# Weighting and folding two of eight value-cache parts on VectorE and GpSimd ahead of TensorE

## The chip, the cores and the metric

One core of a Trainium2 chip runs the whole program. It has five engines with instruction queues of their own: TensorE (PE), VectorE (DVE), ScalarE (ACT), GpSimd (POOL) and SyncE (SP). SP computes nothing here; it issues the loads from the chip's main memory, in the order of the program, and where a load has to wait for its place to come free, everything behind it in SP's queue waits as well. Sixteen DMA engines carry the loads.

The metric is the device time of one execution in microseconds (us), as a median of runs; lower is better.

## The reference

Two layers, run one after the other with the same weights and the same caches. Each is an attention block over a key and a value cache and then a gated MLP, for a batch of 2 and one new token. All data are float32.

```python
def _A_ref(x, k_cache, v_cache, wq, wo):          # B=2, H=32, Sk=8192, Dh=128, D=576
    q = (x @ wq) as (B, H, 1, Dh)
    scores = jnp.einsum("bhqd,bhkd->bhqk", q, k_cache) * (Dh ** -0.5)
    p = _softmax(scores, axis=-1)
    o = jnp.einsum("bhqk,bhkd->bhqd", p, v_cache)
    return (o as (B, 1, H * Dh)) @ wo
...
x = x + _A_ref(_layernorm(x), ...)
x = x + _B_ref(_layernorm(x), ...)                # gelu(x @ w_gate) * (x @ w_up) @ w_down
```

Both caches together hold 2 x 2 x 32 x 8192 x 128 numbers, 537 MB, and each layer reads all of them once, apart from a few parts that are kept on the core between the layers.

## The kernel before

**Items.** Attention walks over items. Items 0 to 29 (`PAIRS` is 30) are pairs: one batch row and two neighbouring heads. Items 30 to 33 (`SINGLE`) are one head each. Layer 0 takes them in rising order, layer 1 in falling order; `seq` is that list. For a pair the keys are 8.4 MB and the values another 8.4 MB. On the core they lie as 128 partitions (64 for each head) with 128 cached positions each, cut into eight parts of `JC` = 16 positions by 128 numbers. K(n) and V(n) below are the keys and values of item n.

**Places.** The buffer `space` has six slots of four parts. A pair's cache takes two neighbouring slots; call slots 0 and 1 place A, 2 and 3 place B, 4 and 5 place C. `Arena.pair` takes, of the places that are wholly free, the one that was freed longest ago. The loads stand in one list (`plan_first` for layer 0) in the order K(0), K(1), V(0), K(2), V(1), K(3), V(2), and so on, and `pump` lets the head of the list go as soon as the program text has passed the point at which a place is freed (`done`). So the order of the program's text decides which place a load gets, and the load's instruction on SP then waits, at run time, for the last work on that place. One load that carries a whole pair's cache is one DMA instruction (line 165). At the end of layer 0 the loads of the single heads have places that are fixed in the plan (lines 338 to 348):

```python
        k(SINGLE[0], (0,))                        # K(30): slot 0
        half(("v", 0, last), vc, last, 0, 1)      # V(29), parts 0 to 3: slot 1
        half(("v", 0, last), vc, last, 4, 5)      # V(29), parts 4 to 7: slot 5
        k(SINGLE[1], (3,))                        # K(31): slot 3
        v(SINGLE[0], (4,))                        # V(30): slot 4
        k(SINGLE[2], (2,))                        # K(32): slot 2
```

**One pair's turn.** In the loop of `attention`, iteration i handles the keys of item n = `seq[i]` in three units of 3, 3 and 2 parts (`units`). For each unit `multiply` has VectorE multiply the keys with the query (line 644; the query lies in PSUM), GpSimd adds the upper half of the products to the lower half (line 661), and `add_up` has VectorE sum what is left into scores (line 664). `add_up` is also what frees the unit's parts. It runs one unit late: the sum of a unit stands on VectorE's queue behind the multiplication of the next unit, and the sum of the third unit stands at the head of the next iteration, followed by `peak` (line 688). `highest` and `softmax` of the item before (p = `seq[i-1]`) follow the first unit's multiplication; `total` (line 729) and `inverse` of p follow the second.

**The values.** Behind the second unit stand, in this order, `gather` of item a = `seq[i-2]` (lines 776 and 777, VectorE), `context` of a, and `values` of item v = `seq[i-1]`. `values` gives TensorE 32 products for a pair (line 762), four for each part: the 8 weight columns of four positions (from `prz`, left there by `softmax`) against those positions' 512 numbers. They accumulate into the four row groups of one PSUM bank, `acc[:, n % 2]`. The last product of a part frees it.

So in steady state of layer 0 K(n+2) takes the place of K(n), which `add_up` frees at the head of iteration n+1, and V(n+1) takes the place of V(n), which `values` frees in iteration n+1: the keys alternate between A and B, and the values stay in C.

Of the kernel before, what the change touches and what calls it, by code (L numbers as in the profile page):

```python
# [9 lines left out]
F32 = mybir.dt.float32  # L10
AF = mybir.ActivationFunctionType
ALU = mybir.AluOpType
# [3 lines left out]
P = 128  # L16
# [3 lines left out]
DH = 128  # L20
# [4 lines left out]
JC = 16  # L25
HALF = P // 2

GH = 4
# [8 lines left out]
PART = JC * DH  # L37
# [4 lines left out]
RING = 5 * SLOT  # L42
END = RING + NPLACE * PLACE
HELD = 5


class Item:
# [12 lines left out]
ITEMS = [Item(b, h, 2) for h in range(0, H - 2, 2) for b in range(B)]  # L60
PAIRS = len(ITEMS)
ITEMS += [Item(b, h, 1) for h in range(H - 2, H) for b in range(B)]
N = len(ITEMS)
# [59 lines left out]
def decode_layers(ctx, tc, x_in, kc, vc, wq, wo, wg, wu, wd, out):  # L123
    nc = tc.nc
    scale = DH ** -0.5

    consts = ctx.enter_context(tc.tile_pool(name="consts", bufs=1))
# [9 lines left out]
    for c in range(4):  # L137
        for s in range(2):
            lo = 32 * c + s * B
# [5 lines left out]
    arena = Arena()  # L145
    queue, ready, places = [], {}, {}

    def pump():
        while queue and queue[0]():
            queue.pop(0)  # L150

    def done(key):
        arena.free(key)
        pump()

    def part_at(at, n):
        return space[:, at:at + n]
# [162 lines left out]
    def name(kind, layer, n):  # L320

        return kind, 1 if n in (KEYS_HELD if kind == "k" else VALUES_HELD) else layer, n
# [126 lines left out]
    side = consts.tile([P, 2], F32, name="side")  # L449
    nc.vector.reduce_sum(side, pick.rearrange("p (s b) -> p s b", s=2), axis=AX.X)  # L450

    strip = consts.tile([P, 4], F32, name="strip")
    nc.vector.reduce_sum(strip, ident.rearrange("p (c r) -> p c r", c=4), axis=AX.X)

# [20 lines left out]
    bank2 = psum1.tile([P, 512], F32, name="bank2")  # L475
    po = bank2[:, 0:2 * GH].rearrange("p (i c) -> p i c", c=2)
    smalls = [bank2[:, 2 * GH + i * P:2 * GH + (i + 1) * P] for i in range(2)]
    kept = psum1.tile([P, JC, DH], F32, name="kept")

    def small(p, n):  # L480

        smalls.append(smalls.pop(0))
        return smalls[0][0:p, 0:n]
# [57 lines left out]
    def attention(layer):  # L541
# [30 lines left out]
        else:  # L572
            half_products(1)
            key = ("wq", 1, NU - 1)
# [7 lines left out]
        seq = list(range(N))[::1 - 2 * layer]  # L582

        def query(n):

            it = ITEMS[n]
            qps.append(qps.pop(0))
            qb[n] = qps[0]
            for i in range(it.heads):
                h, to = it.h + i, slice(i * HALF, i * HALF + P // it.heads)  # L590
                c, r = (h // 4) % 4, h // 16 * B + it.b
                nc.tensor.matmul(  # L592
                    qb[n][to, :], pick[32 * c:32 * c + 4, r:r + 1].to_broadcast([4, P // it.heads]),
                    qsb[32 * c:32 * c + 4, (h % 4) * DH:(h % 4 + 1) * DH], start=True, stop=True,
                )
# [9 lines left out]
        def units(n):  # L605

            if n >= PAIRS or waited(n) or layer == 1 and n == seq[-1]:
                return [(k, 1) for k in range(ITEMS[n].parts)]

            if layer == 1 and n == PAIRS - 2:  # L610
                return [(k, 2) for k in range(0, 8, 2)]
            return [(0, 3), (3, 3), (6, 2)]

        def several(n):
            return units(n)[0][1] > 1
# [70 lines left out]
        def peak(n):  # L686
            m = work.tile([P, 1], F32, name="m")
            nc.vector.reduce_max(m, S[n][:, :ITEMS[n].rows], axis=AX.X)  # L688
            mT[n] = small(1, P)
            nc.tensor.transpose(mT[n], m, ident)  # L690

        def highest(n):

            heads = ITEMS[n].heads
            m1 = work.tile([1, 2], F32, name="m1")
            nc.vector.reduce_max(m1[:, :heads], mT.pop(n).rearrange("p (i q) -> p i q", i=heads), axis=AX.X)  # L696
            mT[n] = small(P, 2)
            nc.tensor.matmul(mT[n][:, :heads], ones[0:1, :], m1[:, :heads], start=True, stop=True)  # L698

        def weights_of(n):  # L700

            if ITEMS[n].heads == 2:
                return prz[:, 2 * (n % 2):2 * (n % 2) + 2, :].rearrange("p a e -> p (a e)")
            return prz[:, n - PAIRS, :]
# [39 lines left out]
        def accumulator(n):  # L744
            return acc[:, n % 2 if n < PAIRS else (n - PAIRS) // B, :]

        def completes(i):

            return seq[i] < PAIRS or i > 0 and ITEMS[seq[i - 1]].h == ITEMS[seq[i]].h

        def values(i, lo=0, hi=8):

            n = seq[i]
            it, key, pr = ITEMS[n], name("v", layer, n), weights_of(n)
            t = ready[key]
            left = not (layer == 0 and n in VALUES_HELD)
            gs = it.rows // 4
            begins = n < PAIRS or not completes(i)
            for g in range(4 * lo, min(gs, 4 * hi)):
                c = g % 4  # L760
                at = 8 * g if it.heads == 2 else 8 * g + 4 - 4 * it.b
                nc.tensor.matmul(  # L762
                    accumulator(n)[32 * c:32 * c + 8, :], pr[:, at:at + 8],
                    t[g // 4][:, g % 4 * 4:g % 4 * 4 + 4, :].rearrange("p j d -> p (j d)"),
                    start=(begins and g < 4), stop=(completes(i) and g >= gs - 4),
                )
                if left and g % 4 == 3:
                    done((key, g // 4))
            if left and 4 * hi >= gs:
                ready.pop(key)  # L770

        def gather(n):

            t = osb[n] = work.tile([P, DH], F32, name="osb")
            q = accumulator(n).rearrange("p (r d) -> p r d", r=4)
            nc.vector.tensor_tensor(out=q, in0=q, in1=diag.unsqueeze(2).to_broadcast([P, 4, DH]), op=ALU.mult)  # L776
            nc.vector.tensor_reduce(out=t, in_=q.rearrange("p r d -> p d r"), axis=AX.X, op=ALU.add)  # L777
# [55 lines left out]
        for i, n in enumerate(seq):  # L833
            last = i == N - 1
            p = seq[i - 1] if i else None

            v = {N - 2: None, N - 1: N - 3}.get(i, i - 1) if layer == 0 else i - 1
            a = seq[i - 2] if i > 1 and completes(i - 2) and not (layer == 0 and last) else None

            soon = layer == 1 and i in (1, 4)  # L840
            first = layer == 1 and i == 1
            us = units(n)

            ahead = p is not None and several(p)
            if first:
                query(seq[i + 1])
            if first or ahead:
                add_up(p, *units(p)[-1])
                peak(p)
            if first:  # L850
                highest(p)
                softmax(p)
            for j, (k, m) in enumerate(us):
                multiply(n, k, m)
                if j == 0 and not last and not first:
                    query(seq[i + 1])
                if at_once(n, k) and k == 0:
                    add_up(n, k, m)
                if j == 1 and first:
                    values(v)  # L860
                    total(p)
                if j == 0 and p is not None and not first and not ahead:
                    add_up(p, *units(p)[-1])
                    peak(p)
                if j == (0 if soon or ahead else 1) and p is not None and not first:
                    highest(p)
                    softmax(p)
                if j == (1 if several(n) else 2) and not first:
                    if p is not None:
                        total(p)  # L870
                        inverse(p)
                    if a is not None:
                        gather(a)
                        if p < PAIRS:
                            context(a)
                    if v is not None and v >= 0:
                        values(v)
                    if a is not None and p >= PAIRS:
                        context(a)
                if j > 0 and (n, us[j - 1][0]) in prod:  # L880
                    add_up(n, *us[j - 1])
                if j == 3 and first:
                    inverse(p)
                if j == (2 if several(n) else 3) and a is not None and p < PAIRS:
                    divide(a, several(n))
                if j == 1 and late is not None:
                    divide(late)
            late = a if a is not None and p >= PAIRS else None
            if layer == 1 and i == 0:

                nc.vector.scalar_tensor_tensor(qsb, acc[:, 0, :], rstd, qsb, op0=ALU.mult, op1=ALU.add)
        n, p = seq[-1], seq[-2]
        add_up(n, *units(n)[-1])
        first, second = groups(layer)[:2]
        if layer == 0:
            values(N - 2)
# [150 lines left out]
```

## Time and profile before

| what | value |
|---|---|
| median of 3 runs | 2686.49 us (2686.27 to 2686.75) |
| span of the profiled execution | 2685.0 us |
| VectorE busy | 1806.0 us, 67% |
| GpSimd busy | 1161.8 us, 43% |
| TensorE busy | 914.4 us, 34% |
| read from main memory | 1153.18 MB, 429 GB/s over the span |

The span is that of one profiled execution on the chip. Busy times are shares of that span and say nothing of waiting; a line like "L644 DVE" is an instruction group of line 644 on VectorE. A row of the timeline gives start, length, engine, line, output and inputs, and in brackets how long the engine had been idle and what released it. Rows with "SPq" are the issues of loads on SP's queue: their time is when the load was handed over, not when its data arrived.

### The profile page before, as it was taken

How to read it: one execution, taken by the hardware profiler on the slowest of the kernel's cores; microseconds unless marked ns; L12 is line 12 of the kernel's file. 1: busy time of each engine (PE TensorE's matmuls, PEld its weight loads, DVE VectorE, ACT ScalarE, POOL GpSimd, SP SyncE). 2: the span in 40 equal slices, each digit the busy share in tenths (PEclk: the TensorE clock that was granted, in tenths of full speed). 3: DMA queues.
4: the chain of work that ended last, by engine and by line, in shares of the span. 5: the costliest groups of instructions: out<-in, count | busy, mean ns of one | idle time of the engine just before them, and what ended most of it. 6: DMA issues, size and time to landing. Idle time of an engine off the chain costs nothing. (4 is left out here: it accounts for less than half of the span.)

```text
span 2685.0 us, 17174 instructions
## 1 busy us (share of the span) xinstructions
PE 914.4 (34%) x7150; PEld 305.4 (11%) x7150; DVE 1806.0 (67%) x874; ACT 163.7 (6%) x786; POOL 1161.8 (43%) x261
## 2 busy tenths in 40 slices
PE   1323332332233233334663333233223323332356
PEld 0100010010001000111221101001000100010022
DVE  4876687677667766867037877667766776776640
ACT  0000000000000000000026000000000000000000
POOL 2543454354445444544028455445444543454420
PEclk7656666665666566566986665666566656656678
DMA  9999999999999999999999999999999999999998
GB/s 422 436 436 426 437 432 434 433 434 432 433 431 435 436 428 433 436 428 425 414 418 434 431 431 436 431 434 434 437 428 434 434 435 431 431 434 435 433 421 375
DMA packets 33950, 1154.30 MB, mean 430 GB/s; under 512 B 4152, under 2 KB 4176, under 8 KB 5968
## 3 DMA queue, kind: packets, MB, share of 16 engines
q1 hardware_dynamic: 33832, 1153.19, 99.8%
q8 instruction: 56, 0.92, 0.1%
q14 instruction: 22, 0.18, 0.0%
q10 hardware_dynamic: 40, 0.01, 0.0%
HBM read 1153.18 MB, written 0.00 MB: 429 GB/s over the span
## 5 line engine op out<-in xcount | busy, mean ns | idle before, releaser
L661 POOL TENSOR_TENSOR space<-space 128x3072 f32<-128x3072 f32 (+3 forms) x221 | 1128.6, 5107 | 1263.3 <-DVE space L644 1202.5
L644 DVE TENSOR_TENSOR space<-space,bank 128x6144 f32<-128x6144 f32 (+3 forms) x223 | 1112.7, 4991 | 560.2 <-DMA space<-in_A_k_cache_dram 496.8
L762 PE MATMUL acc<-space,prz 128*8 128x512 f32 x4096 | 594.6, 744 | 199.4 <-DMA space<-in_A_v_cache_dram 195.5
L664 DVE TENSOR_REDUCE S<-space 128x48 f32<-128x3072 f32 (+3 forms) x223 | 569.3, 2553 | 89.9 <-POOL space L661 89.6
L592 PE MATMUL bank<-qsb,pick 4*64 4x128 f32 (+1 forms) x256 | 46.3, 436 | 863.1 <-DVE space L644 853.1
L762 PEld LDWEIGHTS acc<-space,prz 128*8 128x8 f32 x4096 | 119.1, 104 | 616.3 <-issue 410.6
L784 PE MATMUL bank<-of,osb 128*32 128x2 f32 x512 | 40.9, 202 | 324.4 <-DVE osb L777 324.4
L713 ACT ACTIVATE nbs<-bank 128x2 f32<-128x2 f32 (+1 forms) x68 | 11.6, 171 | 1848.2 <-PE bank L698 1801.8
L592 PEld LDWEIGHTS bank<-qsb,pick 4*64 4x64 f32 (+1 forms) x256 | 20.7, 202 | 882.5 <-DVE space L644 863.2
L517 POOL TENSOR_TENSOR rstd<-ve,mhalf 128x1 f32<-128x1 f32 x4 | 2.2, 550 | 168.8 <-DVE ve L515 168.8
L690 PE MATMUL bank<-ident,m 128*1 128x128 f32 x68 | 19.5, 286 | 160.7 <-DVE m L688 160.5
L784 PEld LDWEIGHTS bank<-of,osb 128*32 128x32 f32 x512 | 35.9, 154 | 331.7 <-DVE osb L777 330.5
L978 DVE STREAM_TRANSPOSE o<-o 128x288 f32<-128x288 f32 x4 | 2.8, 691 | 94.5 <-ACT o L976 94.5
L729 PE MATMUL bank<-sums,unit 128*128 128x2 f32 x120 | 35.2, 363 | 87.0 <-ACT prz L721 87.0
L776 DVE TENSOR_TENSOR acc<-acc,diag 128x512 f32<-128x512 f32 x64 | 43.5, 680 | 22.0 <-PE acc L762 22.0
L721 ACT ACTIVATE prz<-S,nbs 64x128 f32<-64x128 f32 (+1 forms) x128 | 50.7, 396 | 17.3 <-POOL prz L711 14.4
L803 ACT ACTIVATE oT<-bank,rinv 32x8 f32<-32x8 f32 x110 | 28.5, 259 | 381.5 <-PE bank L784 380.8
L654 ACT ACTIVATE space<-space 128x128 f32<-128x128 f32 x164 | 48.3, 296 | 23.6 <-DVE space L644 21.7
L698 PE MATMUL bank<-m,unit 1*128 1x2 f32 (+1 forms) x136 | 39.0, 354 | 25.3 <-DVE m L696 25.3
L777 DVE TENSOR_REDUCE osb<-acc 128x128 f32<-128x512 f32 x64 | 44.3, 691 | 2.2
L521 DVE TENSOR_TENSOR x<-bank,x 128x144 f32<-128x144 f32 x4 | 1.2, 308 | 64.1 <-PE bank L1004 40.4
L729 PEld LDWEIGHTS bank<-sums,unit 128*128 128x128 f32 x120 | 30.1, 311 | 92.2 <-ACT prz L721 92.2
(73 smaller groups left out, 427.6 us busy)
## 6 DMA issues: line engine op xcount, KB each, us to landing
space<-in_A_v_cache_dram SPq DMA_DIRECT2D x8, 4096.0 KB
space<-in_A_k_cache_dram SPq DMA_DIRECT2D x6, 4096.0 KB
space<-in_A_wo_dram SPq DMA_DIRECT2D x15, 1152.0 KB
space<-in_A_k_cache_dram SPq DMA_DIRECT2D x15, 1024.0 KB
space<-in_B_w_down_dram SPq DMA_DIRECT2D x9, 1152.0 KB
space<-in_B_w_gate_dram SPq DMA_DIRECT2D x3, 3456.0 KB
space<-in_A_v_cache_dram SPq DMA_DIRECT2D x10, 1024.0 KB
space<-in_A_wq_dram SPq DMA_DIRECT2D x3, 3072.0 KB
```

The lines of the kernel that those rows point to most:

```text
L592: nc.tensor.matmul(qb[n][to, :], pick[32 * c:32 * c + 4, r:r + 1].to_broadcast([4, P // it.heads]), qsb[32 * c:32 * c + 4, (h % 4) * DH:(h ...
L644: nc.vector.tensor_tensor(out=u[:, :rows, :], in0=t[:, :rows, :], in1=qb[n].unsqueeze(1).to_broadcast([P, rows, DH]), op=ALU.mult)
L654: nc.scalar.activation(u[:, j, :], u[:, j, :], AF.Copy, accum_out=S[n][:, k * JC + j:k * JC + j + 1])
L661: nc.gpsimd.tensor_tensor(out=half, in0=half, in1=u[:, :r, DH // 2:], op=ALU.add)
L664: nc.vector.tensor_reduce(out=S[n][:, k * JC:k * JC + own_rows(n, k, m)], in_=prod.pop((n, k)), axis=AX.X, op=ALU.add)
L698: nc.tensor.matmul(mT[n][:, :heads], ones[0:1, :], m1[:, :heads], start=True, stop=True)
L721: nc.scalar.activation(pr[at, lo:].rearrange("p (g e) -> p g e", e=4)[:, 0:it.rows // 2:2, :], s[at, :it.rows].rearrange("p (g r) -> p g r ...
L729: nc.tensor.matmul(tot[n][:, :ITEMS[n].heads], ones, rs.pop(n), start=True, stop=True)
L762: nc.tensor.matmul(accumulator(n)[32 * c:32 * c + 8, :], pr[:, at:at + 8], t[g // 4][:, g % 4 * 4:g % 4 * 4 + 4, :].rearrange("p j d -> p ...
L776: nc.vector.tensor_tensor(out=q, in0=q, in1=diag.unsqueeze(2).to_broadcast([P, 4, DH]), op=ALU.mult)
L777: nc.vector.tensor_reduce(out=t, in_=q.rearrange("p r d -> p d r"), axis=AX.X, op=ALU.add)
L784: nc.tensor.matmul(po[lo:lo + 32, i, :], t[:, i::GH], of, start=True, stop=True)
```

## The change

For the pairs that `folds` names, the last two parts (`FOLD` = 2, parts 6 and 7, that is 32 of 128 positions) no longer go to TensorE as they are. `weigh` has VectorE add the two weight columns of each position (one is zero) into `share`, 32 numbers for each partition in PSUM, and multiply the 32 x 128 values with them in place. GpSimd then adds halves, 32 rows to 16, to 8, to 4. `folded` gives TensorE one product of these 4 rows, with a constant matrix `owner` that tells the two heads' partitions apart, into the first row group of the same accumulator. `values` gives 24 products instead of 32 and leaves parts 6 and 7 alone; `folded` frees them.

`weigh(a)` stands at the head of iteration i for a = `seq[i-2]`, behind `add_up` and `peak` of p; `folded(a)` stands ahead of `gather(a)`, behind `total` and `inverse` of p, in that same iteration. Both are one iteration later than `values` of that item. `folds` is true for pairs 0 to 27 whose two successors in `seq` have their keys in units of several parts: items 0 to 27 in layer 0 and items 27 down to 3 in layer 1, 53 in all.

```diff
@@ -42,6 +42,7 @@
+FOLD = 2
@@ -449,6 +450,11 @@
+    owner = consts.tile([P, 2, 4], F32, name="owner")
+    nc.vector.memset(owner, 0.0)
+    for i in range(2):
+        nc.vector.memset(owner[i * HALF:(i + 1) * HALF, i, :], 1.0)
@@ -475,6 +481,7 @@
+    share = bank2[:, 2 * GH + 2 * P:2 * GH + 2 * P + FOLD * JC]
@@ -748,13 +755,45 @@
+        def folds(n):
+            i = seq.index(n)
+            return n < PAIRS - 2 and i + 2 < N and several(seq[i + 1]) and several(seq[i + 2])
+
+        def weigh(n):
+            lo = ITEMS[n].parts - FOLD
+            pr = weights_of(n)[:, 2 * JC * lo:2 * JC * (lo + FOLD)].rearrange("p (g a e) -> p a g e", a=2, e=4)
+            nc.vector.tensor_tensor(
+                out=share.rearrange("p (g e) -> p g e", e=4), in0=pr[:, 0], in1=pr[:, 1], op=ALU.add
+            )
+            rows = FOLD * JC
+            t = part_at(arena.live[name("v", layer, n), lo][0], FOLD * PART).rearrange("p (j d) -> p j d", d=DH)
+            nc.vector.tensor_tensor(out=t, in0=t, in1=share.unsqueeze(2).to_broadcast([P, rows, DH]), op=ALU.mult)
+            while rows > 4:
+                rows //= 2
+                nc.gpsimd.tensor_tensor(out=t[:, :rows], in0=t[:, :rows], in1=t[:, rows:2 * rows], op=ALU.add)
+
+        def folded(n):
+            key, lo = name("v", layer, n), ITEMS[n].parts - FOLD
+            nc.tensor.matmul(
+                accumulator(n)[0:8, :], owner.rearrange("p a e -> p (a e)"), part_at(arena.live[key, lo][0], 4 * DH),
+                start=False, stop=True,
+            )
+            for k in range(lo, lo + FOLD):
+                done((key, k))
+            ready.pop(key)
...
-            gs = it.rows // 4
+            gs, less = it.rows // 4, folds(n)
+            if less:
+                gs -= 4 * FOLD
...
-                    start=(begins and g < 4), stop=(completes(i) and g >= gs - 4),
+                    start=(begins and g < 4), stop=(completes(i) and g >= gs - 4 + less),
...
-            if left and 4 * hi >= gs:
+            if left and 4 * hi >= gs and not less:
                 ready.pop(key)
@@ -847,6 +886,8 @@
                 add_up(p, *units(p)[-1])
                 peak(p)
+            if a is not None and folds(a):
+                weigh(a)
             if first:
@@ -870,6 +911,8 @@
                     if a is not None:
+                        if folds(a):
+                            folded(a)
                         gather(a)
```

## The prediction

> **What bounds the kernel now.** I read the page first: slices of the span, then the DMA queues.
>
> ```profile
> span 2685.0 us, 17174 instructions
> DMA  9999999999999999999999999999999999999998
> q1 hardware_dynamic: 33832, 1153.19, 99.8%
> ```
>
> The sixteen DMA engines are busy for 99.8% of the span, from the first slice to the last; no compute engine passes 67%. The kernel is as long as its loads. The 0.2% left are 5.4 us, and they hold the start and the end. So taking work from TensorE can gain nothing, and all that the change can do is to leave the loads without work for a while. What matters is when SP hands each load over against when the load before it ends. One steady period, from the timeline of SP, VectorE, GpSimd and TensorE:
>
> ```profile
> 1024.76 0.33 SPq L165 DMA_DIRECT2D space<-in_A_v_cache_dram  x1
> 1025.57 0.33 SPq L165 DMA_DIRECT2D space<-in_A_k_cache_dram  x1
> ...
> 995.65 6.55 DVE L644 TENSOR_TENSOR space<-space,bank 128x6144 f32<-128x6144 f32 x1 [8.45 <-DMA space<-in_A_k_cache_dram]
> 1023.26 2.29 DVE L664 TENSOR_REDUCE S<-space 128x32 f32<-128x2048 f32 x1 [1.46 <-POOL space L661]
> 1025.58 0.29 DVE L688 TENSOR_REDUCE m<-S 128x1 f32<-128x128 f32 x1
> 1034.35 6.55 DVE L644 TENSOR_TENSOR space<-space,bank 128x6144 f32<-128x6144 f32 x1 [8.48 <-DMA space<-in_A_k_cache_dram]
> 1048.25 0.68 DVE L776 TENSOR_TENSOR acc<-acc,diag 128x512 f32<-128x512 f32 x1
> ...
> 1018.68 4.54 POOL L661 TENSOR_TENSOR space<-space 128x2048 f32<-128x2048 f32 x1 [2.30 <-DVE space L644]
> 1041.03 6.70 POOL L661 TENSOR_TENSOR space<-space 128x3072 f32<-128x3072 f32 x1 [17.81 <-DVE space L644]
> ...
> 1043.44 0.59 PE L729 MATMUL bank<-sums,unit 128*128 128x2 f32 x2 [1.29 <-ACT prz L721]
> 1053.71 2.75 PE L762 MATMUL acc<-space,prz 128*8 128x512 f32 x12 [3.37 <-DMA space<-in_A_v_cache_dram]
> ```
>
> Call the item whose keys arrive at 995.65 n. Keys arrive every 1034.35 - 995.65 = 38.7 us, and V(n) arrives at 1053.71, halfway. VectorE ends item n at 1025.87 and waits 8.5 us for K(n+1). At 1024.76 V(n) is handed over, at 1025.57 K(n+2), while K(n+1) is still under way: two loads stand ready behind the running one.
>
> **The change part by part.**
>
> *Work removed.* Eight of 32 value products for each pair, one added. TensorE waits for the values' load (the row at 1053.71), so this is worth nothing on the path.
>
> *Work added on VectorE and GpSimd.* From the groups of instructions by shape:
>
> ```profile
> L661 POOL TENSOR_TENSOR space<-space 128x2048 f32<-128x2048 f32 x61 | 278.0, 4557 | 145.3 <-DVE space L644 131.8 <-issue 13.5
> L644 DVE TENSOR_TENSOR space<-space,bank 128x4096 f32<-128x4096 f32 x61 | 269.1, 4411 | 0.0
> L661 POOL TENSOR_TENSOR space<-space 128x1024 f32<-128x1024 f32 x24 | 56.5, 2354 | 63.5 <-DVE space L644 62.1 <-DVE rinv L740 1.5
> L648 POOL TENSOR_TENSOR space<-space,qs 128x512 f32<-128x512 f32 x24 | 30.6, 1276 | 17.4 <-ACT qs L643 15.9 <-DMA space<-in_A_k_cache_dram 1.0 <-ACT space L679 0.5
> L776 DVE TENSOR_TENSOR acc<-acc,diag 128x512 f32<-128x512 f32 x64 | 43.5, 680 | 22.0 <-PE acc L762 22.0
> L490 DVE TENSOR_TENSOR apart<-stats,strip 128x24 f32<-128x24 f32 x4 | 0.7, 184 | 0.1
> ```
>
> `weigh` on VectorE: 0.18 us for `share` (the 24-element row) and 4.41 us for 4096 products with one operand in PSUM, as line 644 has it. The new operand repeats each number 128 times in a row instead of a block; line 776 reads its `diag` that way, and 0.68 us for 512 elements fits the same slope ((4.41 - 0.68) / 3584 = 1.04 ns an element). Together 4.6 us: 1025.87 to 1030.5, inside the 8.5 us of waiting. The fold on GpSimd: 4.56 + 2.35 + 1.28 = 8.2 us, 1030.5 to 1038.7; GpSimd is idle from 1023.2 to 1041.03. Both hidden, with 3.9 and 2.3 us to spare; without that cover the 4.6 us would stand once per item, 53 times. `folded` stands behind `total` (1043.44 to 1044.03), so its operand has been ready for 5 us; behind it on TensorE wait only `context` and the next values, and `gather` on VectorE starts at 1048.25 anyway. I take its call as under 0.9 us (12 records of line 762 take 2.75). Nothing on the path.
>
> *Places.* This is the part that counts. V(n) now becomes free only at `folded`, one iteration later and behind the `add_up` that frees K(n+1). So when the head of the list is V(n+1), the free place is that of K(n+1) and not that of V(n); K(n+3) then gets V(n)'s. Every load moves: V(n) lies where K(n) lay, K(n+2) where V(n-1) lay. Hand-over times from the rows above: V(n) needs `add_up` of item n, 1025.55, 0.8 us later than now, and 8.8 us ahead of 1034.35. K(n+2) needs `folded` of n-1, about 1044.9, which is 19 us later than now but still 8.8 us ahead of 1053.71. One load ready behind the running one instead of two, no gap.
>
> How long a load takes to get going I bound by the last one, which has nothing in front of it:
>
> ```profile
> 2682.00 0.64 SPq L1019 DMA_DIRECT2D out_dram<-x  x1
> 2672.00:2676.00 4.00, 3.07 (x73) 1.96 (x66) 0.00 (x0) 0.00 (x0) 0.00 (x0) 1.00 0.86 351
> 2676.00:2680.00 4.00, 2.28 (x54) 1.08 (x48) 0.00 (x0) 0.00 (x0) 0.00 (x0) 1.00 0.51 205
> ```
>
> From 2682.00 to the end of the span at 2685.0 are 3.0 us for start, data and completion: the start is between 0 and 3.0, I take half, 1.5. The Trainium skill (DMA: Bandwidth & Descriptors, Specifications) gives about 0.6 us to the first byte of a load issued as SP does; with that every gap below would be 0.9 us shorter. The two windows of the tail (DMA share 0.86, then 0.51) show that the sixteen engines do not finish together but over some 4 to 8 us.
>
> *Start of layer 0.* Here VectorE is not yet in step.
>
> ```profile
> 92.94 0.33 SPq L165 DMA_DIRECT2D space<-in_A_v_cache_dram  x1
> 101.81 0.33 SPq L165 DMA_DIRECT2D space<-in_A_k_cache_dram  x1
> 103.79 6.55 DVE L644 TENSOR_TENSOR space<-space,bank 128x6144 f32<-128x6144 f32 x1 [1.69 <-DMA space<-in_A_k_cache_dram]
> ```
>
> V(1) moves from 92.94 to where K(3) is now issued, 101.81, since both wait for `add_up` of item 1. K(2) has arrived by 103.79. 101.81 + 1.5 = 103.3: no gap for the engine that finishes last, one or two us for those that finish first. Bounds 0 and 1.1 (with 3.0), I take 0.5. `weigh(0)` then delays item 2 by 101.82 + 0.29 + 4.6 - 103.79 = 2.9 us, within the next loads' lead.
>
> *End of layer 0.* The places now rotate by three: K(2) is in A, K(3) in C, K(4) in B, K(5) in A; K(n) is in A when n leaves 2 on division by 3. So K(29) is in A, where before the change K(28) was. But K(30) has slot 0, a half of A, by the plan.
>
> ```profile
> 1142.00 0.38 SPq L165 DMA_DIRECT2D space<-in_A_k_cache_dram  x1
> 1143.19 36.85 SPq L165 DMA_DIRECT2D space<-in_A_v_cache_dram  x2
> ...
> 1151.92 6.55 DVE L644 TENSOR_TENSOR space<-space,bank 128x6144 f32<-128x6144 f32 x1 [8.44 <-DMA space<-in_A_k_cache_dram]
> 1170.49 4.41 DVE L644 TENSOR_TENSOR space<-space,bank 128x4096 f32<-128x4096 f32 x1
> 1174.82 3.34 DVE L664 TENSOR_REDUCE S<-space 128x48 f32<-128x3072 f32 x1
> 1179.64 2.29 DVE L664 TENSOR_REDUCE S<-space 128x32 f32<-128x2048 f32 x1 [1.47 <-POOL space L661]
> ...
> 1171.29 4.91 PE L762 MATMUL acc<-space,prz 128*8 128x512 f32 x32 [3.28 <-DMA space<-in_A_v_cache_dram]
> ```
>
> K(29) arrives at 1151.92, V(28) behind it at 1171.29. K(30) is the next load; it is now handed over at 1142.00, once parts 0 to 5 of K(28) are summed. After the change it needs the same sum of K(29): 1174.82 + 3.34 = 1178.16. That is 6.9 us after the last load in the queue has arrived, and everything else stands behind it in SP's queue. With 1.5 us to get going the gap is 1178.2 + 1.5 - 1171.3 = 8.4 us for the engine that finishes last; lower bound 6.9 (no delay), upper 9.9 (3.0) plus some 4 us should the end be set by an engine that now finishes early: 13.9. I take 9.0, near the last engine. The loads after it need 1181.93 (sum of K(29)'s third unit) or less, by when K(30) has just begun: no second gap. No later load has slack to give the time back, since the DMA share stays at 9 tenths to the end.
>
> *Layer 1.* Its loads with fixed places precede item 27, where folding begins, and items 2 to 0 at its end do not fold; the places in between rotate freely. Nothing.
>
> *Sum.* 2685.0 + 0.5 + 9.0 = 2694.5 of span; the median of the runs is 1.5 above the span, so 2696.0. The bounds are +6.9 + 0 and +13.9 + 1.1: 2693.4 to 2701.5.
>
> **The rivals.**
>
> *No gap: K(30)'s slot is free in time* (not slower). If the places did not rotate as I worked out, or K(29) lay in B or C, K(30) would go out before 1169.8 (1171.3 less 1.5), and the loads would run through: 2686.5. That time decides. For it speaks that two of three remainders would spare slot 0; against it, that `folded` is in the text one iteration later than the `add_up` that it would have to precede. Much under 2686.5 is not to be had, as the loads fill the span.
>
> *A gap at every load.* With one load in reserve instead of two, each could start late if a hand-over needed more than the 8.8 us of lead. Every us beyond it costs 53 us: at 1 us 2696 + 53 = 2749. Against it: the 3.0 us above, end to end.
>
> *VectorE becomes the bound.* If `weigh` ran at half the rate of line 644 (8.8 us), an item would take 1025.87 - 995.65 + 9.0 = 39.2 us, and some 1 us more since GpSimd then runs past 1041.03, against 38.7: 1.5 x 53 = 80 us less two leads of 8.8, about 2758. The slope of line 776 speaks against it. The Trainium skill (SBUF — State Buffer, Who interferes with whom) says that a VectorE instruction with two SBUF inputs and a GpSimd one that reads SBUF shut each other out; the big product escapes with `share` in PSUM, and the trace agrees, for line 644 takes 6.55 us at 1159.36 beside GpSimd as alone at 1151.92. By it only the 0.18 us sum can be held, while GpSimd is idle: the same 2696.0.
>
> ```profile
> 1158.61 6.70 POOL L661 TENSOR_TENSOR space<-space 128x3072 f32<-128x3072 f32 x1 [17.77 <-DVE space L644]
> 1159.36 6.55 DVE L644 TENSOR_TENSOR space<-space,bank 128x6144 f32<-128x6144 f32 x1 [0.69 <-PE bank L592]
> ```
>
> **How the numbers follow.** My forecast 0.80; no gap 0.10, of which 0.02 for a gain that I do not see; a gap at every load 0.06; VectorE the bound 0.04. About 0.2%, 5.4 us, is what a measurement here can tell from no change. Faster 0.02, same 0.08, slower 0.90. The range holds the forecast's bounds and the small end of a repeated gap: 2692 to 2706.
>
> **What would show it.** Right: the load of K(30) at about 1178 in SP's timeline instead of 1142; a stretch of some 8 us with hardly any DMA between 1171 and 1180; a lower figure in one of the 40 slices, the 18th; K loads some 19 us later against the period elsewhere; the same period of 38.7 us; `weigh` at 4.4 and the fold at 8.2 us inside today's idle times; everything from item 30 on about 9 us later. Wrong: K(30) before 1170, gaps in other slices, or a period over 38.7 us.

## The result, and the profile after

| | before | after |
|---|---|---|
| median of 5 runs | 2686.49 us (2686.27 to 2686.75) | 2698.26 us (2697.55 to 2698.81) |
| span of the profiled execution | 2685.0 us | 2696.8 us |
| VectorE busy | 67% | 76% |
| GpSimd busy | 43% | 59% |
| TensorE busy | 34% | 34% |

The ratio is 1.0043, with a 95% interval of 1.0032 to 1.0054: 11.8 us slower. The page of the changed kernel, in the lines that answer to those of before:

```profile
span 2696.8 us, 16024 instructions
DMA  9999999999999999989999999999999999999998
GB/s 420 420 436 436 434 434 434 433 434 433 433 433 431 434 435 431 433 359 427 420 416 426 436 433 432 434 433 433 433 433 434 434 434 436 428 429 435 435 424 375
q1 hardware_dynamic: 33832, 1153.19, 99.3%
```

The same row of the kernel before:

```profile
GB/s 422 436 436 426 437 432 434 433 434 432 433 431 435 436 428 433 436 428 425 414 418 434 431 431 436 431 434 434 437 428 434 434 435 431 431 434 435 433 421 375
```

The loads moved the same bytes with the same packets, and were busy for 99.3% of the span instead of 99.8%. One slice of the forty stands out, the 18th (1146 to 1214 us): 359 GB/s among slices of 431 to 435 before it. That is where layer 0 ends. The second slice, in which V(1) is loaded, is low as well: 420 instead of 436. Everywhere else the rate is within some 10 GB/s of what it was.

The timeline of SP's queue in the changed kernel, at the start and at the end of layer 0. The file's lines have moved: loads are issued at line 166 now, keys are multiplied at 651, halved on GpSimd at 668 and summed at 671, the values' products stand at 801.

```profile
72.95 0.33 SPq L166 DMA_DIRECT2D space<-in_A_k_cache_dram  x1
101.77 0.33 SPq L166 DMA_DIRECT2D space<-in_A_v_cache_dram  x1
118.67 0.33 SPq L166 DMA_DIRECT2D space<-in_A_k_cache_dram  x1
...
1104.74 0.33 SPq L166 DMA_DIRECT2D space<-in_A_v_cache_dram  x1
1125.02 0.33 SPq L166 DMA_DIRECT2D space<-in_A_k_cache_dram  x1
1143.44 0.33 SPq L166 DMA_DIRECT2D space<-in_A_v_cache_dram  x1
1178.99 0.33 SPq L166 DMA_DIRECT2D space<-in_A_k_cache_dram  x1
1182.75 0.82 SPq L166 DMA_DIRECT2D space<-in_A_v_cache_dram  x2
```

V(1) goes out at 101.77, where it went at 92.94. The pattern of two loads in quick succession has become one load every 19 us. K(30) goes out at 1178.99 instead of 1142.00. What it waited for, and what had run dry by then, from the timeline of VectorE:

```profile
1152.72 6.55 DVE L651 TENSOR_TENSOR space<-space,bank 128x6144 f32<-128x6144 f32 x1 [3.78 <-DMA space<-in_A_k_cache_dram]
1175.62 3.35 DVE L671 TENSOR_REDUCE S<-space 128x48 f32<-128x3072 f32 x1
1191.33 2.29 DVE L651 TENSOR_TENSOR space<-space,bank 128x2048 f32<-128x2048 f32 x1 [8.28 <-DMA space<-in_A_k_cache_dram]
```

and from TensorE's, the first product with V(28):

```profile
1172.08 9.82 PE L801 MATMUL acc<-space,prz 128*8 128x512 f32 x64 [3.27 <-DMA space<-in_A_v_cache_dram]
```

The sum of parts 3 to 5 of K(29) ends at 1175.62 + 3.35 = 1178.97, and K(30) goes out 0.02 us later. V(28), the last load in the queue, was there by 1172.08. VectorE then stands still for 8.28 us and begins K(30) at 1191.33. In the kernel before it came to K(30) 9.2 us earlier, straight from its other work and with no wait for the load:

```profile
1182.16 2.28 DVE L644 TENSOR_TENSOR space<-space,bank 128x2048 f32<-128x2048 f32 x1
```

The gap itself, in windows of 4 us (after the length come the engines' busy times with counts, the clock, the DMA share, and GB/s):

```profile
1164.00:1168.00 4.00, 0.00 (x0) 0.00 (x0) 3.96 (x4) 0.00 (x0) 3.32 (x2) 0.50 0.80 344
1168.00:1172.00 4.00, 0.64 (x8) 0.56 (x8) 4.00 (x3) 0.52 (x2) 4.00 (x1) 0.50 0.27 115
1172.00:1176.00 4.00, 3.92 (x20) 0.73 (x24) 4.00 (x2) 0.00 (x0) 1.63 (x2) 0.50 0.02 4
1176.00:1180.00 4.00, 4.00 (x32) 0.80 (x28) 2.96 (x1) 0.00 (x0) 4.00 (x1) 0.79 0.09 25
1180.00:1184.00 4.00, 2.17 (x21) 0.38 (x13) 2.57 (x2) 0.00 (x0) 0.40 (x1) 1.00 0.97 369
```

A window counts a packet where it begins, and most packets take 2.4 us. The DMA share is already down to 0.80 and 0.27 before 1172: most of the sixteen engines run dry ahead of the last one. The kept trace shows this directly. Each load reports sixteen completions, which I take as one for each engine; those of V(28) lie between 1168.11 and 1172.03, at 1170.04 on average. All engines then stand still to nearly 1180. The shares of the five windows sum to 2.15, that is 8.6 us of work in 20 us, where the same windows of the kernel before hold 19.8; two of them:

```profile
1168.00:1172.00 4.00, 0.72 (x5) 0.12 (x8) 4.00 (x2) 0.52 (x2) 4.00 (x1) 0.50 0.93 401
1172.00:1176.00 4.00, 4.00 (x32) 0.86 (x28) 4.00 (x2) 0.00 (x0) 1.70 (x2) 0.76 1.01 430
```

The work that was added stands where it was expected. The groups by shape (lines 767 and 772 are `weigh`, 775 the fold, 780 `folded`):

```profile
L775 POOL TENSOR_TENSOR space<-space 128x2048 f32<-128x2048 f32 x53 | 238.6, 4502 | 417.8 <-DVE space L772 417.8
L772 DVE TENSOR_TENSOR space<-space,bank 128x4096 f32<-128x4096 f32 x53 | 234.3, 4420 | 1.8
L780 PE MATMUL acc<-space,owner 128*8 128x512 f32 x106 | 99.2, 1038 | 0.0
L767 DVE TENSOR_TENSOR bank<-prz 128x32 f32<-128x32 f32 x53 | 10.6, 200 | 26.8 <-PE bank L697 26.8
```

One fold, from the timeline of all engines around the arrival of K(29):

```profile
1144.29 0.20 DVE L767 TENSOR_TENSOR bank<-prz 128x32 f32<-128x32 f32 x1 [0.56 <-PE bank L697]
1144.52 4.42 DVE L772 TENSOR_TENSOR space<-space,bank 128x4096 f32<-128x4096 f32 x1
1149.02 8.28 POOL L775 TENSOR_TENSOR space<-space 128x2048 f32<-128x2048 f32 x3 [7.93 <-DVE space L772]
1159.41 6.70 POOL L668 TENSOR_TENSOR space<-space 128x3072 f32<-128x3072 f32 x1 [2.10 <-issue]
1161.97 1.87 PE L780 MATMUL acc<-space,owner 128*8 128x512 f32 x2
```

4.42 us on VectorE, 8.28 us on GpSimd, done 2.1 us before GpSimd is needed for the next keys; VectorE still waits 3.78 us for K(29) behind it (the row at 1152.72).

### The profile page after: what moved, and what is told of

Its sections match the earlier page's. It is cut to its first block, busy times and chain, and to the rows that moved or that the text cites. A ratio compares the mean times of both kernels' runs of the same rounds, so it can differ in the third digit from the quotient of the medians.

```text
span 2696.8 us, 16024 instructions
## 1 busy us (share of the span) xinstructions
PE 920.2 (34%) x6408; PEld 288.6 (11%) x6408; DVE 2051.1 (76%) x983; ACT 163.8 (6%) x786; POOL 1592.4 (59%) x420
## 3 DMA queue, kind: packets, MB, share of 16 engines
q1 hardware_dynamic: 33832, 1153.19, 99.3%
## 5 line engine op out<-in xcount | busy, mean ns | idle before, releaser
L775 POOL TENSOR_TENSOR space<-space 128x2048 f32<-128x2048 f32 x159 | 430.9, 2710 | 426.1 <-DVE space L772 417.8
L801 PE MATMUL acc<-space,prz 128*8 128x512 f32 x3248 | 503.9, 784 | 201.4 <-DMA space<-in_A_v_cache_dram 197.4
L772 DVE TENSOR_TENSOR space<-space,bank 128x4096 f32<-128x4096 f32 x53 | 234.3, 4420 | 1.8
L801 PEld LDWEIGHTS acc<-space,prz 128*8 128x8 f32 x3248 | 97.5, 107 | 549.8 <-issue 341.8
L780 PE MATMUL acc<-space,owner 128*8 128x512 f32 x106 | 99.2, 1038 | 0.0
```

Source lines behind the costliest of these rows:

```text
L772: nc.vector.tensor_tensor(out=t, in0=t, in1=share.unsqueeze(2).to_broadcast([P, rows, DH]), op=ALU.mult)
L775: nc.gpsimd.tensor_tensor(out=t[:, :rows], in0=t[:, :rows], in1=t[:, rows:2 * rows], op=ALU.add)
L780: nc.tensor.matmul(accumulator(n)[0:8, :], owner.rearrange("p a e -> p (a e)"), part_at(arena.live[key, lo][0], 4 * DH), start=False, stop ...
L801: nc.tensor.matmul(accumulator(n)[32 * c:32 * c + 8, :], pr[:, at:at + 8], t[g // 4][:, g % 4 * 4:g % 4 * 4 + 4, :].rearrange("p j d -> p ...
```

## The experiments

The theory: the added work is hidden and the removed work was hidden too; the 11.8 us are two gaps in the stream of loads, and both come from the order in which the program's text frees its places, a small one in front of V(1) and a large one in front of K(30). The rival that had to be taken seriously is that the folding itself costs something, some 0.22 us for each of 53 folds.

**e1: fold from item 4 on.** The rotation of the places begins later, and the place that it has reached by item 29 is another.

```diff
-            return n < PAIRS - 2 and i + 2 < N and several(seq[i + 1]) and several(seq[i + 2])
+            return (layer == 1 or n >= 4) and n < PAIRS - 2 and i + 2 < N and several(seq[i + 1]) and several(seq[i + 2])
```

> Layer 0 folds from item 4 on instead of item 0 (49 folds instead of 53). Theory (two gaps in the loads, made by the order of the places): the rotation then puts K(29) in place B and V(27) in A, so K(30)'s slot 0 is freed by the values of item 27, an iteration early: K(30) goes out by 1145, V(29)'s first half by 1165, no gap, and V(1) goes out at 93 again: 2686.5 (2686 to 2687.5). Rival (the folding itself costs, some 0.22 us for each of 53): 2686.5 + 49 x 0.22 = 2697.3.

Measured: 2686.41 us, ratio 0.9999 (0.9990 to 1.0008). SP's queue in it:

```profile
92.57 0.33 SPq L166 DMA_DIRECT2D space<-in_A_v_cache_dram  x1
...
1142.12 0.38 SPq L166 DMA_DIRECT2D space<-in_A_k_cache_dram  x1
1161.62 17.30 SPq L166 DMA_DIRECT2D space<-in_A_v_cache_dram  x2
```

V(1) at 92.57, K(30) at 1142.12, V(29)'s first half at 1161.62, all well ahead of the end of the load before: no gap. 49 of the 53 folds are still there and cost nothing that can be measured. One number in `folds` takes the whole loss away, so a cost per fold is out. The same kernel, run again beside e9:

> The kernel of e1 once more on this chip, as the reference for e9: 2686.5 if e1's equality with the kernel before holds; 2687 or more if it was chance.

Measured: 2686.42 us, ratio 0.9999 (0.9990 to 1.0008).

**e2: fold from item 1 on** (the same line, `n >= 1`). Only the start of layer 0 falls into place; the end does not.

> Layer 0 folds from item 1 on (52 folds). Theory: the places fall as in the changed kernel at the end of layer 0 (K(29) in A), so K(30) still waits for the sum of K(29)'s parts 3 to 5, at about 1178, and the gap there stays, 10.6 us as the mean of the DMA engines; the gap at the start (1.0 us) is gone, since V(1) gets the place of V(0) at 93: 2697.3 (2696.5 to 2697.8). Rival (cost per fold): 2698.0.

Measured: 2697.14 us, ratio 1.0038 (1.0026 to 1.0051). Against the changed kernel that is 1.1 us less, and against the kernel before 10.6 us more. This is not yet the size of each gap: the packet records of the traces, in the next section, give 1.6 us for the one in front of V(1) and 10.6 for the one in front of K(30) in the changed kernel, and 10.1 for the latter here. SP's queue and, below it, TensorE's first product with V(28):

```profile
92.60 0.33 SPq L166 DMA_DIRECT2D space<-in_A_v_cache_dram  x1
...
1176.71 0.33 SPq L166 DMA_DIRECT2D space<-in_A_k_cache_dram  x1
```

```profile
1170.55 8.34 PE L801 MATMUL acc<-space,prz 128*8 128x512 f32 x64 [4.02 <-DMA space<-in_A_v_cache_dram]
```

**e3: fold from item 3 on** (`n >= 3`). Here V(28) comes to lie in A, and K(30) waits for products instead of a sum.

> Layer 0 folds from item 3 on (50 folds). Theory: the rotation puts V(28) in A, so K(30) waits for the last value product of item 28 (about 1180 to 1181) instead of the sum of K(29) at 1178: the gap is 1.5 to 3 us longer than with folding from item 1: 2698.5 to 2700.3, with three folds less than the changed kernel. Rival (cost per fold): 2697.6, under the changed kernel.

Measured: 2695.06 us, ratio 1.0030 (1.0019 to 1.0041). Both expectations missed: less than the changed kernel, not more, and less than a cost per fold would give. K(30) went out at 1175.76, not at 1180. The same two views:

```profile
1175.76 0.33 SPq L166 DMA_DIRECT2D space<-in_A_k_cache_dram  x1
```

```profile
1169.96 9.17 PE L801 MATMUL acc<-space,prz 128*8 128x512 f32 x64 [3.28 <-DMA space<-in_A_v_cache_dram]
```

The mistake was mine: slot 0 holds only the first half of V(28), so K(30) waits for the 16th of its 32 products and not for the last. From V(28)'s arrival to the hand-over are 1175.76 - 1169.96 = 5.8 us here and 6.2 in e2 (1176.71 against 1170.55), so the shorter gap has the shorter time, by 2.1 us where 0.4 to 1.0 are seen at the hand-over. By the packets the gap itself is 0.8 us shorter; the profiled execution of e2 also leaves its DMA engines idle for 1.4 us between 1375 and 1400 us, in the MLP of layer 0, which e3's does not. Why, and whether e2's other runs do, is not shown.

**e4: no folding work, only the late release.** All 32 products stay, nothing is weighted; parts 6 and 7 are declared free where `folded` stood.

```diff
-            if a is not None and folds(a):
-                weigh(a)
...
-            nc.tensor.matmul(accumulator(n)[0:8, :], owner..., start=False, stop=True)
             for k in range(lo, lo + FOLD):
                 done((key, k))
...
-            if less:
-                gs -= 4 * FOLD
...
-                if left and g % 4 == 3:
+                if left and g % 4 == 3 and not (less and g // 4 >= it.parts - FOLD):
```

> No folding work at all: all 32 value products stay on TensorE, and nothing is weighted; only the text's point at which parts 6 and 7 are declared free is moved to where the change has it, one iteration later. Theory: the places rotate as in the changed kernel, both gaps are there: 2698.3 (2697.3 to 2698.8), with K(30) at about 1179. Rival (cost of the folding work): 2686.5.

Measured: 2699.34 us, ratio 1.0050 (1.0037 to 1.0062), half a microsecond above the range that I gave. SP's queue:

```profile
101.98 0.33 SPq L166 DMA_DIRECT2D space<-in_A_v_cache_dram  x1
...
1180.15 0.33 SPq L166 DMA_DIRECT2D space<-in_A_k_cache_dram  x1
```

The whole loss is there without the folding: of what the change adds to VectorE and GpSimd, only the three instructions that fill `owner` once at the start are left (877 on VectorE instead of 874). Together with e1, work without loss and loss without work, this settles the cause: the place in the text at which two parts are freed.

**e5: all 53 folds, with other fixed places.** The other way to mend it leaves the rotation alone and moves the places of the plan to what the rotation has free.

```diff
-        k(SINGLE[0], (0,))
-        half(("v", 0, last), vc, last, 0, 1)
-        half(("v", 0, last), vc, last, 4, 5)
+        k(SINGLE[0], (4,))
+        half(("v", 0, last), vc, last, 0, 5)
+        half(("v", 0, last), vc, last, 4, 1)
...
-        v(SINGLE[0], (4,))
+        v(SINGLE[0], (0,))
```

> The changed kernel with all 53 folds and its rotation, but with the fixed places at the end of layer 0 laid where the rotation leaves room: K(30) in slot 4, V(29)'s halves in slots 5 and 1, V(30) in slot 0. Theory: K(30) now waits only for values of item 27 and goes out right behind V(28), at about 1144; the gap at the end of layer 0 is gone, the gap of 1.0 us at the start stays: 2687.6 (2687 to 2688.7). Rival (the folding costs time by itself, the places only shift where it shows): near 2698.

Measured: 2689.24 us, ratio 1.0009 (1.0000 to 1.0018). The large gap is gone, but 0.5 us more are left than I allowed for. The new plan has made a gap of its own: K(33), in slot 0 now behind V(30), waits for the values of item 30. Its hand-over on SP, and the windows around it with a DMA share of 0.80 and 0.89:

```profile
1228.12 0.33 SPq L166 DMA_DIRECT2D space<-in_A_k_cache_dram  x1
```

```profile
1224.00:1228.00 4.00, 4.00 (x31) 0.95 (x24) 2.91 (x2) 0.00 (x0) 2.08 (x1) 0.70 0.80 340
1228.00:1232.00 4.00, 0.47 (x12) 0.38 (x7) 1.21 (x1) 0.00 (x0) 0.30 (x1) 1.00 0.89 311
```

**e9: as e5, with V(31) ahead of K(33) in the list.**

```diff
-        k(SINGLE[3], (0,))
-        v(SINGLE[1], (4,))
+        v(SINGLE[1], (4,))
+        k(SINGLE[3], (0,))
```

> As e5, with the loads of V(31) and K(33) exchanged in the list: V(31), whose slot 4 comes free with the sum of K(30), goes out first, and K(33), which has to wait in slot 0 for the values of item 30, runs behind it with 9 us more of lead. Theory: e5's excess over 2687.6 was a third gap, of its own making, in front of K(33) (hand-over at 1228.1, DMA share 0.80 and 0.89 around it); without it the gap of 1.0 us at the start alone remains: 2687.6 (2687.1 to 2688.3). Rival (folding all 53 costs some 2.5 us apart from gaps): 2689.2.

Measured: 2688.58 us (11 runs, 2687.60 to 2689.98), ratio 1.0007 (0.9998 to 1.0016). Less than e5, in the direction expected, but 0.3 us above the range. Against the kernel before, timed beside it (2686.75), it is 1.8 us, about what the gap in front of V(1) costs by the packets (1.6 us, next section). By the packets, too, the DMA engines stand idle for 1.1 us between 1215 and 1250 us in e5, and not at all here, so the gap in front of K(33) is gone; the difference between the two times, 0.7 us, is less than what the runs of either scatter by.

**e6: a longer gap.** K(30) and V(29)'s first half exchange their slots, so that K(30) needs the sum of K(29)'s third unit.

```diff
-        k(SINGLE[0], (0,))
-        half(("v", 0, last), vc, last, 0, 1)
+        k(SINGLE[0], (1,))
+        half(("v", 0, last), vc, last, 0, 0)
```

> The changed kernel with K(30) and V(29)'s first half exchanged: K(30) in slot 1, which holds parts 4 to 7 of K(29). Theory: K(30) then waits for the sum of K(29)'s third unit, at 1182.7 instead of 1179.0, and the gap grows by those 3.7 us: 2698.3 + 3.7 = 2702.0 (2701 to 2703). If instead only the engine that finishes last counts, or the time is made up behind the gap: under 2700.5.

Measured: 2701.96 us, ratio 1.0056 (1.0044 to 1.0069). SP's queue:

```profile
1182.57 0.33 SPq L166 DMA_DIRECT2D space<-in_A_k_cache_dram  x1
```

K(30) goes out 1182.57 - 1178.99 = 3.6 us later, and the kernel takes 2701.96 - 2698.26 = 3.7 us longer. A microsecond more of gap costs a microsecond more at the end; nothing behind it gives that back.

**e7: the removed products by themselves.** The kernel before, without the eight products.

```diff
+            few = n < PAIRS - 2
             for g in range(4 * lo, min(gs, 4 * hi)):
...
-                nc.tensor.matmul(...)
+                if not few or g < gs - 8:
+                    nc.tensor.matmul(...)        # stop four groups from the last one kept
```

> The kernel before, with the eight value products of parts 6 and 7 of pairs 0 to 27 left out (their share of the attention is missing), their parts freed at the same points as before. Theory: TensorE is not on the path and the loads fill the span: 2686.5 (2686.0 to 2687.0). Rival (the removed products are worth something that the change gives back elsewhere): about 2.4 us for each of 56 turns would be 134 us at most; anything under 2685.

Measured: 2686.46 us, ratio 0.9999 (0.9990 to 1.0008). TensorE's busy time fell from 914.4 to 818.8 us, and the time did not move. The page:

```profile
span 2685.2 us, 15380 instructions
PE 818.8 (30%) x6254; PEld 282.6 (11%) x6254; DVE 1806.1 (67%) x874; ACT 163.8 (6%) x786; POOL 1161.6 (43%) x261
```

**e8: how much room VectorE has left.** e1's kernel with the large product of `weigh` done twice.

```diff
+            nc.vector.tensor_tensor(out=t, in0=t, in1=share.unsqueeze(2).to_broadcast([P, rows, DH]), op=ALU.mult)
```

> Folding from item 4 on in layer 0 (no gap from the places, 2686.4), with the product of the values and their weights on VectorE done twice (the weights enter squared for parts 6 and 7): 4.42 us more in each of 49 folds. Theory (VectorE has about 3.4 us left in a turn of 38.7): each turn takes 1.0 us too long, the lead of the loads of about 7 us is used up after some 7 items of each layer, and from then on every turn costs 1.0: (24 - 7) + (25 - 7) = 35 us: 2721 (2710 to 2740). Rival (VectorE has room for it, since its idle time is only a wait): 2686.4.

Measured: 2726.76 us, ratio 1.0149 (1.0135 to 1.0163). Two turns from VectorE's timeline:

```profile
935.83 6.55 DVE L651 TENSOR_TENSOR space<-space,bank 128x6144 f32<-128x6144 f32 x1
...
975.59 6.55 DVE L651 TENSOR_TENSOR space<-space,bank 128x6144 f32<-128x6144 f32 x1
```

The keys are multiplied every 975.59 - 935.83 = 39.8 us, with no wait for a load in front: VectorE sets the pace, 1.1 us over 38.7. So the cover that hides `weigh` is real and, behind `weigh`, 3.4 us deep: 4.4 us for each fold cost nothing, and another 4.4 us cost 40 us in all. The lead of the loads, which I took as seven turns in each layer, paid for fewer: 40.3 / 1.06 = 38 of the 49 turns are charged.

## Why the prediction held, and what was off in it

**What bounds the kernel.** Right. The removed products alone gain nothing (e7), and the time follows the gaps in the loads (e6).

**The work added.** Right in size and place: 4.42 us predicted as 4.41, 8.28 as 8.2, both in idle time (e1). Two sizes were off without effect. `folded` takes 1.87 us, not under 0.9: its two records are 1038 ns each on average; the granted clock in the window behind it is 0.50. And `share` waits 0.56 us for TensorE's transposition of the maximum (line 697), which lies in the same PSUM bank, a wait that I had not listed. VectorE keeps 3.3 to 3.8 us of room instead of 3.9.

**The rotation of the places.** Right step by step: K(30) waits for the sum of parts 3 to 5 of K(29), predicted at 1178.2, seen at 1178.97; V(1) goes out at 101.77; K loads elsewhere come 19 to 21 us later against the period, without a gap; one slice, the 18th, shows it.

**The size of the two gaps.** Both were taken too small. Between them lie the 2.3 us from 2696.0 to 2698.26. The packets of the kept traces (start, length and bytes of each) measure the gaps without going by any one row. The table says how much later than in the kernel before the loads had moved their first 500 MB (1159 us there, ahead of the gap at K(30)), 520 MB (1205 us, behind it) and 1150 MB (2670 us, near the end). It rests on one execution of each kernel.

| later than before, us | 500 MB | 520 MB | 1150 MB |
|---|---|---|---|
| the changed kernel | 1.6 | 12.2 | 11.7 |
| e1 | -0.2 | 0.0 | -0.6 |
| e2 | 0.0 | 10.1 | 10.7 |
| e3 | 0.0 | 9.3 | 8.1 |
| e4 | 2.1 | 13.6 | 12.4 |
| e5 | 1.9 | 1.4 | 2.5 |
| e6 | 1.6 | 15.7 | 14.8 |
| e9 | 1.6 | 1.4 | 1.0 |

In the changed kernel the gap in front of V(1) is 1.6 us, taken as 0.5 with an upper bound of 1.1, and the gap in front of K(30) is 12.2 - 1.6 = 10.6, taken as 9.0. The 0.5 us less near the end are no more than e1 shows without a gap. Both times I stayed near the engine that finishes last, 8.4 and 0, on the ground that it sets the end. For that engine the 8.4 came out: the last packet of V(28) ends at 1171.57, the first of K(30) begins at 1179.97. (It begins 1.0 us after the hand-over, where I had allowed 1.5 us; the other 0.5 are between the end of V(28)'s last packet and the product that waits for it, at 1172.08.) But the engines that had finished early lost more, and the time follows the mean.

From the mean of V(28)'s completions to the hand-over of K(30) are 7.3 us in e3, 8.3 in e2, 9.0 in the changed kernel, 9.6 in e4 and 12.6 in e6, and the gaps of the table are 9.3, 10.1, 10.6, 11.5 and 14.1: 1.6 to 2.0 longer each time. Counted from the last completion the difference scatters more, from 3.4 to 4.5. The windows above give 19.8 - 8.6 = 11.2 us, near this too; they count a packet whole where it begins. The upper bound of 13.9 had held the reason; the value chosen in it was too low.

"Everything from item 30 on about 9 us later" holds for VectorE's start of K(30), 9.2 us, since VectorE itself was late there in the kernel before, but not for the loads, which run 12 us late.

**The rivals.** No gap at K(30): refuted by the row at 1178.99, though e1 shows how near it was, since folding from item 4 on would have made it true. A gap at every load: not seen; one load in reserve is enough at 8.8 us of lead. VectorE as the bound: not at one pass, but e8 reaches it with a second, at about the price that its arithmetic gave for a turn.

No version beats the kernel before. e1 equals it, and with the loads at 99.8% of the span there is nothing left for this change to win.

## What to carry to other kernels

Where loads fill the span, ask of a change first where it moves the release of a buffer, and follow the allocator through to the loads whose places are fixed by hand: two parts of eight freed one iteration later turned an alternation of two places into a rotation of three, and the loss came 28 items later, where the loads with fixed places begin. Read a wait in SP's queue together with what is still under way: the lead between the hand-over and the end of the running load is the quantity that counts, and a gap costs its full length. For the length, take the mean over the DMA engines and not the moment at which the last one lands.

## What the runs showed of the hardware that was not expected

The sixteen DMA engines do not stay abreast. In the kernel before, the sixteen completions of one early load lie between 82.56 and 83.16 us, those of V(28) between 1166.45 and 1171.25: 0.6 us and 4.8 us. Without a gap that costs nothing. In front of one the mean engine is done 2.0 us ahead of the last (1170.04 and 1172.03 in the changed kernel), and the row that waits for the landing shows only the last. The gap brings the engines together again: K(30)'s completions lie between 1190.55 and 1191.30.

A sum of 32 elements on VectorE (line 767) waited 0.56 us in each of 53 turns (26.8 us in all) for a TensorE write to another part of the same PSUM bank. In the kept trace it waits on the semaphore that this write raises, so it is the program that orders the two; whether the chip would need it was not tried.
